# A fused attention and two MLP stages on one core: pooled scores, exponentials, copies, zero products, v pooling and query loads put in another order

## The chip, the core and the metric

The kernel runs on one core of a Trainium2 chip. The metric is the device time of one execution in microseconds, taken as the median of several runs. TensorE is called PE here, its weight loads PEld, VectorE DVE, ScalarE ACT, GpSimd POOL, and SyncE, which issues the loads, SP.

## What is computed

```python
def _attn_ref(q, k, v):            # q, k, v: (2, 8, 576, 64)
    factor = 4; Sd = S // factor   # 144 pooled positions
    q_d, k_d, v_d = (mean over each 4 neighbouring positions of q, k, v)
    out_up = np.repeat(softmax(scale * q_d @ k_d.T) @ v_d, factor, axis=2)
    mask = np.abs(pos[:, None] - pos[None, :]) < factor
    out_local = softmax(where(mask, scale * q @ k.T, -1e9)) @ v
    return out_up + out_local

def reference(...):
    x = attention output as (1152, 512)
    h = x @ w_in                   # 512 -> 2048
    x = (h * clip(h + 3, 0, 6) / 6) @ w_out
    p = domain_probs / domain_probs.sum(-1)
    return sum over 4 experts e of p[:, e] * (relu(x @ w1[e]) @ w2[e])
```

So each head has a local attention (a band of 7 keys) and a pooled one over 144 positions; their sum goes through a gated MLP and then through four dense experts.

## The kernel before, in words

Attention works on 8 units (`Unit`): a unit is one pair of heads of one batch, the two heads on the two halves of the 128 partitions. The loop over `t` (lines 1146 to 1216) is a software pipeline written out by hand: `manual_schedule` keeps the order in which the code issues instructions on every engine, and each engine works its own queue in that order. In turn `t` stand the scores of unit `t`, the turning (transposition by PE) of unit `t-1`, and the products with v of unit `t-2`; the pooling of k and q (`sums`) runs two units ahead.

The steps of a unit, with their lines. `masks` (699): a count of products of zeros (L654, results unused, the count from `IDLE` and `AHEAD_OF`) and the mask as a first product (L703). `scores` (711): 18 windows of 32 queries, 36 matmul instructions (L715). `pooled_scores` (769): L775. `pooled_softmax` (783): DVE takes the maximum (L793, tile mxd) and scales it (L795, nm), ACT does four exponentials with a sum each (L805, eight instructions, tile exd). `less_max` (728): DVE maximum L733 and subtraction L734 (tile ex), ACT exponential L740. `normalise` (742): DVE L745 and L747, POOL multiplies (L749). `pooled_normalise` (814): DVE L816 and L820, POOL multiplies (L821). `turn` (753): PE L759, then ACT copies the result out (L766, L767, tile aT). `pooled_turn` (828): PE L834, ACT copies (L842, tile aTd). `values` (844): 72 matmul instructions (L854). `pooled_values` (863): PE L870, ACT copy pd (L878), DVE sum xf (L884), ACT high part of x (L892); `low` (898): DVE L900. `sums` (661): POOL additions (L510 is the helper's line), for the first units DVE L683.

PSUM: `single()` (163) hands out six banks in turn, so a bank is free again only when what was read from the sixth tile before it has been read; the pooled scores have a double bank of their own (`pair()`). `pool_v(b, idle, cols)` (518) pools half of the columns of v of one batch: `idle` zero products, 36 matmul instructions (L530), two ACT copies (L538). `POOLS` (123) says in which turns; the first half of batch 0 is pooled in turn 1 behind `turn`.

Queries lie in four tiles, and `Q_AT` (48) says which unit uses which; one half of each head's rows must be zero (`clear_q`, 425). Units 0 to 3 get theirs through a loaded slot and two copies (`put_q`, 429; ACT and DVE, lines 421 and 423). Units 4 to 7 are loaded straight into the tile (`load_direct`, 457, four small loads a unit). The loads stand in a list (562 to 586) with the turn from which each may be issued; `load` (196) lets SP wait so that a limited number of bytes is under way. `convert` steps the conversion of the first MLP's weights (227) on ACT and DVE in turns 3 and up. Slots of 8 KB a partition are shared by all of this (`take`, `give`). Two turns after the last unit drain the pipeline (t = 8 and 9), mixed with the first pieces of the MLP (`pieces`, PE lines 410 to 412).

## Time and profile before

| | us |
|---|---|
| median of 3 runs (lowest, highest) | 646.23 (646.16, 647.0) |
| the profiled execution | 647.11 |
| its span in the trace | 645.4 |
| PE busy in the span | 636.8 (99%) |
| DVE busy | 422.4 (65%) |
| ACT busy | 259.5 (40%) |
| POOL busy | 101.2 (16%) |

The attention fills about the first tenth of the span, the two MLPs the rest. In the page's 40 slices PE's busy tenths read 8 in the first, 7 in the last and 9 in all between. The profile's page shows busy shares for the whole span; a share in it is an average over stages with different limits, so what stops the attention has to be read from that stretch alone: from the waits of PE, the order of instructions in time, and the granted clock of PE in each stretch. In the timeline a row gives the start, the time of all instructions merged in the row, engine, line of the code, operation, the tiles written and read, and in brackets the idle time before it with what ended it.

### The profile page before, as it was taken

Reading aid. Unit: us, or ns where it says so; the run is one execution under the profiler, and the core shown is the slowest. Engines: PE = TensorE matmul, PEld = TensorE weight load, DVE = VectorE, ACT = ScalarE, POOL = GpSimd, SP = SyncE. Lnnn points to the kernel's source line nnn. Section 1 sums busy time; section 2 is a strip of 40 time slices with the busy share of each in tenths; the row PEclk is TensorE's granted clock in tenths of the full one; section 3 lists DMA queues with packets and bytes.
Section 4 is the critical chain, followed back from the end, with each engine's and each line's share of the span. In section 5 each row is a group of like instructions: output and inputs, shape, how many; then the busy total and the mean of one; then the engine's idle time right before and its main releaser. Section 6 shows DMA issues by size and latency. Waiting matters only on the chain.

```text
span 645.4 us, 11490 instructions
## 1 busy us (share of the span) xinstructions
PE 636.8 (99%) x4637; PEld 582.6 (90%) x4637; DVE 422.4 (65%) x837; ACT 259.5 (40%) x605; POOL 101.2 (16%) x152
## 2 busy tenths in 40 slices
PE   8999999999999999999999999999999999999997
PEld 4676999999999999998998998998998998988986
DVE  7877899862695238585665665665765755755742
ACT  7767577442564246343223233232341341431310
POOL 5873000000000053201201201201201201201000
PEclk9898999999999999999999999999999999999999
DMA  8876434300420011300110110120210300300012
GB/s 247 207 190 197 133 121 141 131 1 1 171 91 0 1 66 67 131 2 1 66 66 0 67 66 1 66 67 1 72 59 1 113 20 9 123 1 0 2 50 98
DMA packets 24861, 45.86 MB, mean 71 GB/s; under 512 B 11228, under 2 KB 16616, under 8 KB 21352
## 3 DMA queue, kind: packets, MB, share of 16 engines
q1 hardware_dynamic: 24808, 45.13, 21.7%
q8 instruction: 36, 0.59, 0.4%
q14 instruction: 17, 0.14, 0.1%
HBM read 42.76 MB, written 2.36 MB: 70 GB/s over the span
## 4 chain that ended last, share of the span: by engine, by line
PE 93%; DVE 3%; ACT 3%; issue 0%; ACTq 0%; DVEq 0%
PE bank L1051 28%; PE bank L410 10%; PE bank L412 10%; PE bank L411 10%; PE bank L1313 10%; PE bank L1314 10%; PE bank L1312 10%; ACT exd L805 1%; PE pair L854 1%; PE pair L715 1%; PE pair L870 1%; ACT q L421 1%; PE pair L530 1%; DVE mxd L793 1%; PE pair L775 0%; PE pair L654 0%
## 5 line engine op out<-in xcount | busy, mean ns | idle before, releaser
L1051 PEld LDWEIGHTS bank<-xop,slot 128*128 128x128 f32 x1344 | 179.5, 188 | 1.2
L1051 PE MATMUL bank<-xop,slot 128*128 128x288 f32 x1344 | 180.3, 294 | 0.0
L1313 PE MATMUL bank<-slot,h 128*128 128x512 f32 x288 | 112.2, 390 | 0.0
L1312 PE MATMUL bank<-slot,h 128*128 128x512 f32 x288 | 112.1, 389 | 0.0
L1314 PE MATMUL bank<-slot,h 128*128 128x512 f32 x288 | 112.1, 389 | 0.0
L1320 DVE SCALAR_TENSOR_TENSOR slot<-bank,pr,slot 128x512 f32<-128x512 f32 x63 | 47.3, 751 | 80.6 <-PE bank L1314 80.6
L510 POOL TENSOR_TENSOR st<-slot 128x256 f32<-128x256 f32 x16 | 14.0, 872 | 460.8 <-DMA slot<-in_w_dram 231.7
L410 PE MATMUL bank<-x,slot 128*128 128x384 f32 x192 | 64.4, 336 | 0.0
L1314 PEld LDWEIGHTS bank<-slot,h 128*128 128x128 f32 x288 | 54.1, 188 | 11.3
L412 PE MATMUL bank<-x,slot 128*128 128x384 f32 x192 | 64.2, 334 | 0.0
L411 PE MATMUL bank<-x,slot 128*128 128x384 f32 x192 | 64.1, 334 | 0.0
L410 PE MATMUL bank<-h,slot 128*128 128x384 f32 x192 | 64.1, 334 | 0.0
L411 PE MATMUL bank<-h,slot 128*128 128x384 f32 x192 | 64.1, 334 | 0.0
L412 PE MATMUL bank<-h,slot 128*128 128x384 f32 x192 | 64.1, 334 | 0.0
L1312 PEld LDWEIGHTS bank<-slot,h 128*128 128x128 f32 x288 | 54.1, 188 | 10.7
L1313 PEld LDWEIGHTS bank<-slot,h 128*128 128x128 f32 x288 | 54.1, 188 | 10.7
L510 DVE TENSOR_TENSOR u<-bank,u 128x288 f32<-128x288 f32 x96 | 43.6, 454 | 19.7 <-PE bank L1051 19.3
L1080 ACT ACTIVATE h<-c 128x288 fp32r<-128x288 f32 x64 | 27.7, 445 | 71.3 <-DVE c L510 71.3
L340 ACT ACTIVATE slot<-st 128x512 fp32r<-128x512 f32 x32 | 19.2, 626 | 63.2 <-POOL st L334 63.2
L931 ACT ACTIVATE t<-bank,half__190 128x384 f32<-128x384 f32 x48 | 27.7, 582 | 40.3 <-PE bank L412 40.2
L932 DVE SCALAR_TENSOR_TENSOR slot<-t,bank 128x384 f32<-128x384 f32 x48 | 26.3, 552 | 25.1 <-ACT t L931 25.0
L940 DVE TENSOR_TENSOR h<-slot,h 128x384 fp32r<-128x384 f32 x48 | 27.1, 577 | 23.4 <-ACT h L939 23.3
(111 smaller groups left out, 935.3 us busy)
## 6 DMA issues: line engine op xcount, KB each, us to landing
slot<-in_w_dram SPq DMA_DIRECT2D x16, 1024.0 KB, 4.8
slot<-in_w_out_dram SPq DMA_DIRECT2D x8, 1024.0 KB, 4.8
slot<-in_w_in_dram SPq DMA_DIRECT2D x20, 256.0 KB, 4.0
slot<-in_v_dram SPq DMA_DIRECT2D x12, 256.0 KB, 3.8
slot<-in_w_in_dram SPq DMA_DIRECT2D x3, 1024.0 KB, 4.9
slot<-in_kT_dram SPq DMA_DIRECT2D x8, 288.0 KB, 3.3
out_dram<-slot SPq DMA_DIRECT2D x9, 256.0 KB, 2.0
slot<-in_qT_dram SPq DMA_DIRECT2D x4, 288.0 KB, 3.5
```

The lines of the kernel that those rows point to most:

```text
L410: nc.tensor.matmul(ps, wh, xh, start=first, stop=False)
L411: nc.tensor.matmul(ps, wh, xl, start=False, stop=False)
L412: nc.tensor.matmul(ps, wl, xh, start=False, stop=last)
L510: eng.tensor_tensor(out=out, in0=a, in1=b, op=ALU.add)
L931: nc.scalar.activation(out=t, in_=ps, func=AF.Relu, bias=half_, scale=1.0 / (6.0 * UP))
L940: nc.vector.tensor_tensor(out=g[:, 1, :], in0=u, in1=r32(g[:, 0, :]), op=ALU.subtract)
L1051: nc.tensor.matmul(ps, a[:, i, k], b[:, j, k], start=start and k == 0 and n == 0, stop=stop and k == 1 and n == 2, skip_group_check=True,)
L1080: nc.scalar.activation(out=self.h[:, 0, i, j], in_=of, func=AF.Relu)
L1312: nc.tensor.matmul(ps, hh, w[:, 0], start=(f == 0), stop=False)
L1313: nc.tensor.matmul(ps, hh, w[:, 1], start=False, stop=False)
L1314: nc.tensor.matmul(ps, hl, w[:, 0], start=False, stop=(f == NF - 1))
L1320: nc.vector.scalar_tensor_tensor(out=to, in0=ps, scalar=share, in1=to, op0=ALU.mult, op1=ALU.add)
```

## The change

Pooled scores, the maximum of them and the exponentials are split (`pooled_max`, `pooled_exps`). In turns 1 to 7 the pooled scores now stand behind the values of unit `t-2`, the exponentials behind the pooled values, and the high part of x (`high`) behind the exponentials. The pooled normalisation of unit `t-1` moves from the end of its own turn to the following turn, behind `less_max`. `sums` moves to the end of the turn. v's first half is pooled in turn 1 ahead of `turn`, with four zero products in place of two. `AHEAD_OF` gives the mask of turn 2 three zero products, those of turns 4 to 7 one. Units 4 and 5 get their queries through a slot and copies (`pair < 3`), only units 6 and 7 directly, now into tiles 2 and 3; all loads may be issued from the start.

```diff
--- before.py
+++ after.py
@@ -45,7 +45,7 @@
 NWIN = S // QB
 NI = 5
 NA = 2 * NI - 1
-Q_AT = (0, 1, 0, 1, 2, 3, 0, 1)
+Q_AT = (0, 1, 0, 1, 0, 1, 2, 3)
 NP = 3
 W = QB + 2 * (FACTOR - 1)
 WP = 64
@@ -118,11 +118,12 @@
 
 LEFT, RIGHT, BEFORE_H, AFTER = 64, 480, 256, 384
 BEFORE_X = 448
-
-
-POOLS = {4: (0, 1), 6: (1, 0), 7: (1, 1)}
+FIRST_IDLE = 4
+
+
+POOLS = {1: (0, 0), 4: (0, 1), 6: (1, 0), 7: (1, 1)}
 SPARE = {}
-AHEAD_OF = {2: 2, 3: 2, 4: 2, 5: 2, 6: 2, 7: 2, 1: 4}
+AHEAD_OF = {2: 3, 3: 2, 4: 1, 5: 1, 6: 1, 7: 1, 1: 4}
 
 
 JS = 2
@@ -436,7 +437,7 @@
         b, hp = divmod(2 * pair + at, NHP)
         if pair not in k_slots:
             k_slots[pair] = take()
-            if pair < 2:
+            if pair < 3:
                 q_slots[pair] = take()
         k = k_slots[pair][0][:, at * SK : (at + n) * SK].rearrange("p (u s) -> p u s", u=n)
         for edge in (slice(0, FACTOR - 1), slice(SK - FACTOR + 1, SK)):
@@ -468,7 +469,7 @@
 
     def load_qk(pair, at=0, n=2):
         load_k(pair, at, n)
-        if pair < 2:
+        if pair < 3:
             load_q(pair, at, n)
         else:
             load_direct(2 * pair + at)
@@ -574,8 +575,8 @@
         (0, lambda: load_v(0, 0, COLS[1])),
         (0, lambda: load_v(0, 1, COLS[1])),
         (0, lambda: load_v(0, 2, COLS[1])),
-        (3, lambda: load_qk(3, 0, 1)),
-        (4, lambda: load_qk(3, 1, 1)),
+        (0, lambda: load_qk(3, 0, 1)),
+        (0, lambda: load_qk(3, 1, 1)),
         (0, lambda: load_v(1, 0, COLS[0])),
         (0, lambda: load_v(1, 1, COLS[0])),
         (0, lambda: load_v(1, 2, COLS[0])),
@@ -657,6 +658,7 @@
         def __init__(self, u):
             self.u = u
             self.b, self.hp = divmod(u, NHP)
+            self.scale = SCALE / FACTOR**2
 
         def sums(self):
 
@@ -685,7 +687,7 @@
                     two = k2[:, r, : NI - r]
                     add(nc.gpsimd, to, two[:, :, :, 0], two[:, :, :, 1])
             half = k[:, room].rearrange("p (j f) -> p j f", f=2)
-            if pair < 2:
+            if pair < 3:
                 of = q_slots[pair][0][:, o * S : (o + 1) * S].rearrange("p (j f) -> p j f", f=FACTOR)
                 add(nc.gpsimd, half, of[:, :, 0:2], of[:, :, 2:4])
             else:
@@ -722,7 +724,7 @@
 
             if self.u % 2:
                 give(k_slots.pop(self.u // 2))
-                if self.u < NHP:
+                if self.u < 2 * 3:
                     give(q_slots.pop(self.u // 2))
 
         def less_max(self):
@@ -780,9 +782,9 @@
                         stop=True,
                     )
 
-        def pooled_softmax(self):
-
-            scale = SCALE / FACTOR**2
+        def pooled_max(self):
+
+            scale = self.scale
             mx = att.tile([KC, 2, 2], F32, tag="mxd", name="mxd", bufs=2)
             if self.both is None:
                 of = [(mx[:, h], self.sd[h][:KC, : 2 * PK]) for h in range(2)]
@@ -791,7 +793,7 @@
             for to, src in of:
                 src = src.rearrange("p (i w) -> p i w" if src.ndim == 2 else "p h (i w) -> p h i w", w=PK)
                 nc.vector.tensor_reduce(out=to, in_=src, op=ALU.max, axis=AX.X)
-            nm = att.tile([KC, 4], F32, tag="nm", name="nm", bufs=3)
+            self.nm = nm = att.tile([KC, 4], F32, tag="nm", name="nm", bufs=3)
             nc.vector.tensor_scalar(
                 out=nm,
                 in0=mx.rearrange("p h i -> p (h i)"),
@@ -799,6 +801,8 @@
                 scalar2=None,
                 op0=ALU.mult,
             )
+
+        def pooled_exps(self):
             self.exd = att.tile([KC, 4, PK], F32, tag="exd", name="exd", bufs=2)
             self.smd = sm = att.tile([KC, 4], F32, tag="smd", name="smd", bufs=3)
             for n in range(4):
@@ -806,8 +810,8 @@
                     out=self.exd[:, n, :],
                     in_=self.sd[n // 2][:KC, n % 2 * PK : (n % 2 + 1) * PK],
                     func=AF.Exp,
-                    bias=nm[:, n : n + 1],
-                    scale=scale,
+                    bias=self.nm[:, n : n + 1],
+                    scale=self.scale,
                     accum_out=sm[:, n : n + 1],
                 )
 
@@ -889,11 +893,13 @@
                     .to_broadcast([P, n, nj, FACTOR]),
                     op=ALU.add,
                 )
-            nc.scalar.activation(out=hi, in_=self.xf, func=AF.Copy)
             self.hl = hi, lo
             if hp == NHP - 1:
                 for s in v_slots[b].values():
                     give(s)
+
+        def high(self):
+            nc.scalar.activation(out=self.hl[0], in_=self.xf, func=AF.Copy)
 
         def low(self):
             hi, lo = self.hl
@@ -1160,55 +1166,62 @@
                 n.pooled_scores()
                 n.less_max()
                 units[1].sums()
-                n.pooled_softmax()
+                n.pooled_max()
+                n.pooled_exps()
                 n.normalise()
             else:
                 n.masks(AHEAD_OF.get(t, 0))
-                if t == 2:
+                if 1 < t < 2 * 3 - 1:
                     put_q(nc.scalar, t + 1, 0)
                     put_q(nc.vector, t + 1, 1)
-                n.pooled_scores()
                 n.scores()
                 load_next(t + 1)
-                n.pooled_softmax()
-                if t == 1:
-                    units[0].pooled_normalise()
-                    units[2].sums()
                 n.less_max()
+        if 1 <= t <= NU:
+            units[t - 1].pooled_normalise()
+        if t == 1:
+            units[2].sums()
         if 2 < t < NU + 1:
             units[t - 3].low()
         if 0 < t < NU:
             n.normalise()
-            n.pooled_normalise()
         if t == 1:
             put_q(nc.scalar, t + 1, 0)
             put_q(nc.vector, t + 1, 1)
         if t in (1, 2):
-            clear_q(nc.scalar, t + 3, 0)
-            clear_q(nc.vector, t + 3, 1)
-        if 0 < t < NU - 2:
-            units[t + 2].sums()
+            u = 2 * 3 + (1, 2).index(t)
+            clear_q(nc.scalar, u, 0)
+            clear_q(nc.vector, u, 1)
         if t == NU:
             pieces(1)
         if t >= NU:
             units[t - 2].values()
             units[t - 2].pooled_values()
+            units[t - 2].high()
         if t > NU:
             pieces(1)
             units[t - 3].low()
             units[t - 2].low()
         if t in POOLS:
             b, part = POOLS[t]
-            pool_v(b, 0, COLS[part])
+            pool_v(b, FIRST_IDLE if t == 1 else 0, COLS[part])
         if 1 <= t <= NU:
             units[t - 1].turn()
         if 2 <= t < NU:
             units[t - 2].values()
+        if 1 <= t < NU:
+            n.pooled_scores()
+            n.pooled_max()
+        if 2 <= t < NU:
             units[t - 2].pooled_values()
-        if t == 1:
-            pool_v(0, 2, COLS[0])
+        if 1 <= t < NU:
+            n.pooled_exps()
+        if 2 <= t < NU:
+            units[t - 2].high()
         if 1 <= t <= NU:
             units[t - 1].pooled_turn()
+        if 0 < t < NU - 2:
+            units[t + 2].sums()
         convert(3 if t >= NU else {3: 2, 4: 1, 5: 1, 6: 1, 7: 1}.get(t, 0))
         if t in ():
             load_to(loaded[0])
```

## Rows read from the trace of the kernel before

**Rows 1.** Waits of PE, 0 to 72 us: waiter, awaited, total us, times, longest.

```profile
PE pair L654 <- ACT aT L766: 0.6, 2, 0.4
PE pair L854 <- DVE ex L734: 1.1, 1, 1.1
PE pair L715 <- ACT q L421: 0.9, 1, 0.9
PE pair L759 <- POOL ex L749: 0.5, 1, 0.5
```

**Rows 2.** Timeline of PE in turn 5: start, us, engine, line, operation.

```profile
38.02 0.60 PE L654 MATMUL pair<-zeros 128*128 128x512 bf16 x2
38.46 0.31 PE L703 MATMUL pair<-mask,identb 128*128 128x342 bf16 x1
38.70 0.71 PE L775 MATMUL pair<-slot 64*72 64x144 f32 x8
39.34 1.25 PE L715 MATMUL pair<-slot,q 128*64 128x38 f32 x36
40.52 0.76 PE L759 MATMUL pair<-ident,ex 128*128 128x128 f32 x5
41.21 1.35 PE L854 MATMUL pair<-aT,slot 38*64 38x32 f32 x72
42.50 0.86 PE L870 MATMUL pair<-aTd,slot 80*64 80x144 f32 x8
43.29 0.70 PE L834 MATMUL pair<-ident,exd 72*80 72x72 f32 x8
43.97 0.59 PE L654 MATMUL pair<-zeros 128*128 128x512 bf16 x2
```

**Rows 3.** Timeline of PE in turns 1 and 4.

```profile
8.55 1.04 PE L654 MATMUL pair<-zeros 128*128 128x512 bf16 x4
...
13.49 1.93 PE L530 MATMUL pair<-slot,fours 38*32 38x256 f32 x36
...
28.83 0.91 PE L654 MATMUL pair<-zeros 128*128 128x512 bf16 x2 [0.38 <-ACT aT L766]
...
32.86 1.93 PE L530 MATMUL pair<-slot,fours 38*32 38x256 f32 x36
```

**Rows 4.** Stretches: length, busy PE, PEld, DVE, ACT, POOL; PE clock; DMA share; GB/s.

```profile
28.80:31.00 2.20, 2.17 (x11) 1.04 (x10) 1.99 (x7) 1.10 (x4) 1.68 (x2) 0.54 0.73 194
38.00:44.00 6.00, 6.00 (x144) 4.54 (x143) 5.47 (x10) 3.76 (x15) 3.56 (x6) 1.00 0.71 201
52.50:55.50 3.00, 3.00 (x21) 1.71 (x19) 2.45 (x5) 2.00 (x6) 1.74 (x2) 0.56 0.81 262
```

**Rows 5.** Chain that ended last, in turn 5: start, us, what.

```profile
40.11 0.68 DVE mxd L793
...
41.51 1.55 ACT exd L805 x8
43.06 0.39 ACT ex L740
```

**Rows 6.** Timeline of POOL, DVE and ACT, turns 2 to 5.

```profile
16.96 0.98 POOL L749 TENSOR_TENSOR ex<-ex,rec 128x342 f32<-128x342 f32 x1
19.01 2.56 POOL L510 TENSOR_TENSOR slot<-slot 128x288 f32<-128x288 f32 x5
22.22 0.99 DVE L423 CAST q<-zeros 64x576 f32<-64x576 bf16 x1
24.00 0.48 DVE L492 MEMSET slot<- 3x512 f32 x1
45.35 0.68 ACT L892 ACTIVATE x<-xf 128x576 fp32r<-128x576 f32 x1 [1.10 <-DVE xf L884]
45.94 0.68 ACT L842 ACTIVATE aTd<-pair 80x288 f32<-80x288 f32 x2
```

**Rows 7.** Timeline of SP's queue: the first loads of v.

```profile
2.70 5.10 SPq L198 DMA_DIRECT2D slot<-in_v_dram  x9
```

**Rows 8.** The page's DMA issues: count, size, median us from issue to landing.

```profile
slot<-in_v_dram SPq DMA_DIRECT2D x12, 256.0 KB, 3.8
```

## The prediction, made before the changed kernel ran

> **What bounds the kernel now.** I read the page first: TensorE (PE) is busy almost through the whole span and the chain of work that ended last runs on it. Behind the attention the two MLPs keep PE at nine tenths or more of every slice but the last, so only the first slices, the eight turns of attention, are open. There I read three views. The waits of PE up to 72 us [rows 1] name what stopped it: 1.1 us once in the middle of the value products (L854) for DVE's subtraction L734, 0.6 us in two pieces at a turn's first zero product (L654) for the copy L766, 0.5 us at L759 and 0.9 us at the very start (L715). The timeline of turn 5 [rows 2] shows a turn that nothing stopped: two zero products 0.44 us, mask 0.24, scores 1.18 (L715), turn 0.69 (L759), values 1.29 (L854), pooled values 0.79 (L870), pooled turn 0.68 (L834), and pooled scores 0.64 (L775): 5.95 us from 38.02 to 43.97. So a turn is bound by PE's own work, and what can be won is only what lies above these 5.95 us. The third view, the stretches with their granted clock [rows 4], shows the rest: twice the clock is near half of full (0.54 at 28.8 us, 0.56 at 52.5 us), so the lower of the two levels, 1.2 instead of 2.4 GHz. Each time PE had just stood still: 0.38 us ahead of the 28.83 us product [rows 3], and the 1.1 us of [rows 1] shortly before 52.5 us. What one fall costs is read from turn 4: from its first zero product to the end of its scores it takes 32.86 - 28.83 = 4.03 us [rows 3], in turn 5 the same work takes 40.52 - 38.02 = 2.50 us [rows 2]: 1.5 us a fall, 3.0 us for two.
>
> **The change part by part.**
>
> *Pooled scores behind the values.* The turn's first bank is freed by the copies L766, and in the kernel before these stand in ACT's queue behind eight exponential steps that need the pooled scores of the same turn. In the new order ACT's local exponential and L766 come first. PE does as much as before. The two waits for L766 (0.6) go, since those copies now need nothing later than the scores. The 1.1 us wait for L734 goes: in the kernel before DVE had the pooled maximum and its scaling (together 41.51 - 40.11 = 1.40 us to the first exponential, [rows 5]) ahead of the maximum and subtraction of the scores; both now stand behind the subtraction. The 0.5 us at L759 goes because v is now pooled ahead of the first turn: that work, 1.93 us long [rows 3], fills the time in which the normalised exponentials come. Removed: 0.6 + 1.1 + 0.5 = 2.2 us. The 0.9 us at the start stay.
>
> What comes in their place has three parts.
>
> (a) *The pooled normalisation L821 and its reader are now in one turn.* POOL is in order: L749(1), then the sums of unit 3, then L821 of unit 1. L749 begins at 16.96 and takes 0.98, the five sums take 2.56, and L821 some 1.07 (it is what lies between the end of L749 at 17.94 and the sums at 19.01) [rows 6]: 16.96 + 0.98 + 2.56 + 1.07 = 21.57. PE: from 8.55 [rows 3] four zeros 0.88, mask 0.24, scores 1.18, four zeros 0.88, pooling 1.9, turn 0.69, pooled scores 0.64, pooled turn 0.68: 15.6; then three zeros 0.66, mask 0.24, scores 1.18, turn 0.69, values 1.29, pooled scores 0.64, pooled values 0.79: 21.1 is where the pooled turn of unit 1 wants L821. So a wait of 0.5, less whatever PE is late by. Bounds 0 (PE late by as much) to 1.0 (POOL late by as much again); I take 0.3, since (c) makes PE some 0.2 late. In later turns L821 waits for DVE's denominators, which stand behind the subtraction: with 1.40 for the maximum and what follows it (an estimate, by the pooled maximum of [rows 5]) and 1.07 it is done 2.5 us after the scores, PE asks for it 0.69 + 1.29 + 0.64 + 0.79 = 3.4 us after them: no wait, 0.9 us to spare.
>
> (b) *The second bank of the values is freed by the first copy L842 of the pooled turn one turn earlier*, which now stands last on ACT. From the pooled scores' end: maximum to last exponential 43.06 - 40.11 = 2.95 us [rows 5], the copy to x (L892, behind it now) some 0.6, half of the two copies L842 0.34 [rows 6]: 3.9. PE from the same point: pooled values 0.79, pooled turn 0.68, one or two zeros 0.22 or 0.44, mask 0.24, scores 1.18, turn 0.69: 3.8 or 4.0. So nothing to spare, in the turns without pooling of v, 3 and 5 (in 4, 6 and 7 the pooling gives 1.9 us more). In turn 3 the clearing of a query tile (0.99, [rows 6]) stands ahead of that maximum on DVE. Bounds 0 to 1.0 together (below nothing can't be: it is a wait); I take 0.4, nearest to the half of the clearing.
>
> (c) *v pooled ahead of the first turn.* PE asks for v at 8.55 + 0.88 + 0.24 + 1.18 + 0.88 = 11.7. The nine loads are issued by 7.8 and such a load lands 3.8 after its issue [rows 7, 8]: 11.6. The wait is 0 at least and 13.49 - 11.7 = 1.8 at most, since at 13.49 the kernel before did this work without a wait [rows 3]. I take 0.2.
>
> *Fewer zeros.* Counted from the tables: before 11 + 4 + 6 x 2 + 2 = 29 zero products, after 11 + 4 + 4 + 3 + 2 + 4 x 1 = 28. One at 0.22 us [rows 2]: 0.2 us less. The last four turns have one each and no more; what that does to the clock is weighed below.
>
> *Direct loads for the last queries alone, all loads issued at the start.* Units 4 and 5 get their queries through a slot and two copies each (ACT and DVE, in turns 3 and 4), in place of eight small direct loads. PE has no wait for a load in [rows 1], so earlier loads win nothing there; and the copies stand at a turn's head, ahead of a subtraction that is waiting for scores, where both engines are idle: nothing on PE. Without that cover each would delay L766 by some 0.7 us, as long as the copy L892 of the same size [rows 6], and in these turns there is more than that to spare. On POOL the sums of units 4 and 5 become whole-width ones: no longer than those of unit 3. The slots' edges of the last pair are filled at the start on POOL, ahead of the constants, and two fills of v's slots (0.48 each, [rows 6]) on DVE ahead of the mask: that part of PE's start has the 0.9 us wait for the queries behind it, so 0 to 0.1; I take 0. On SP no issue waits for scores any more.
>
> **The sum** against the profiled execution, 647.11 us with a span of 645.40: removed 2.2 of waits, 0.2 of zeros, 3.0 of low clock if it never falls; added 0.3 + 0.4 + 0.2 = 0.9. That is -4.5. The waits that stay are of the length of the 0.38 us pause ahead of the fall at 28.8 us, and the one in turn 3 stands among the value products, as the 1.1 us pause did. So I keep one fall, +1.5: **-3.0 us**, 644.1 for such a profiled execution. The median of the runs is 646.23, 0.9 below the profiled one; taken off there as well: **643.2**. What is won before 62 us reaches the end if the weights' conversion keeps up: it hangs on PE's last turns and moves along with them.
>
> **The clock, and what the Trainium skill says of it.** The row that speaks for less cover: from 38.0 to 44.0 PE ran without a pause, from 39.3 on without a zero product [rows 2], and the clock stayed at 1.00 [rows 4]. The Trainium skill, "TensorE: Matmul & The Clock Gate", Part 1, "What's actually happening", says that the low clock is the default and that activity releases it; that speaks against taking zero products out. In the same page "A second HAM failure mode: psum-queue depth-cycling" says that short idles between groups of matmuls, as PSUM banks are cycled, make the clock swing; by that the falls go with the waits. By the first alone the sum would end at rival 2, by the second at rival 1.
>
> **The rivals.** (1) *No fall at all*: the three remaining waits are too short. -4.5: 641.7. For: of the two pauses at L654, 0.6 us together, the shorter brought no fall [rows 1]. Against: the longer, 0.38, did [rows 3]. (2) *The clock falls oftener (slower).* With one zero product in each of the last four turns, a short wait anywhere in a turn brings the clock down, as the 0.38 us did. Each fall costs 1.5, so three eat the 4.5 and it decides from the fourth: 646.23 - 4.5 + 6.0 = 647.7; five give 649.2. For: both falls began in a turn's stretch from the values to the next zero products. Against: the stretch from 38 to 44 us [rows 2, 4]. (3) *A new wait in each turn takes the place of the old ones*: L821 or L842 is late by 0.5 in six turns, and both falls stay: 2.2 + 0.2 go, 3.0 come, 646.8. For: (b) has nothing to spare. Against: PE's being late gives time to the others, so that such a wait doesn't add up. (4) *Two falls as before*, -1.5: 644.7. That the loads' part does nothing is in the sum already.
>
> **How the numbers follow.** One fall left, 643.2: 0.34. None, 641.7: 0.28. Two, 644.7: 0.15. Three falls or new waits, about 646.2 to 646.8: 0.11. Slower by the clock, 647.7 and up: 0.12. A measurement of this kernel can tell 0.2% (1.3 us) from no change: faster is the first three less a little, 0.75; same 0.13; slower 0.12. The range: downwards all that is removed and none of the added waits, 646.23 - 5.4 = 640.8; upwards to 646.0, which takes in two falls with the upper bounds of (a) and (b), and leaves out the last two cases.
>
> **What would show it.** Right: in the waits of PE L654 for L766 and L854 for L734 are gone; PE's first MLP product comes some 3 us earlier; at most one stretch of half clock before it; short waits at L834 for L821 and at L854 for L842. Wrong: a longer wait for v at L530; three or more stretches of half clock; a wait of 0.5 us for L842 or L821 in each turn; a wait of PE behind 72 us for a converted weight.

## The result, and the profile after

The changed kernel takes 642.87 us (median of 20 executions, 641.96 to 670.23); the kernel before, run beside it, 652.35 (20 executions, 644.57 to 657.12). The ratio is 0.9887, with a 95% interval from 0.9849 to 0.9924. It is a ratio of means, and like the ratios further down it leaves out each execution that is more than 1.5% above the fastest of its kernel: here all 8 of the changed kernel above 650 us (655.83 to 670.23), but only 2 of the 11 of the kernel before. Over all 20 executions each, the means are 652.1 and 650.5. So the usual execution became faster, the mean of all did not.

Both medians hide a spread that the three runs ahead of the prediction (646.16 to 647.0) did not show: single executions of either kernel differ by how long the granted clock of PE stays at its lower level (at a mean clock of 1.00 the kernel before takes 644.60 to 644.75, at 0.995 646.9 to 647.5, at 0.984 653.6 to 654.0), so each comparison below says which clock it is at. At 1.00 the changed kernel takes 641.94 to 642.54 in most executions: 644.60 - 641.94 = 2.7 us less from lowest to lowest.

The profile that came with the result is of an execution of 670.23 us, with a long stretch of low clock. The same kernel profiled once more took 641.94 us, with a span of 640.2 and PE busy for 632.5 of it; that one stands against the profiled execution of before (647.11, span 645.4). From turn 1's first zero product to the first MLP product it takes 56.89 - 8.79 = 48.10 us; in the kernel before it was 62.18 - 8.55 = 53.63 (8.55 in [rows 3]; 62.18 is the start of its first product at L410). So 5.5 us are won there, 0.24 are lost ahead of it, and the span is 5.2 shorter. The profiled execution of before has its two falls of the clock in that stretch [rows 4], this one has none.

The waits of PE up to 110 us in the profile of 641.94 us (waiter, awaited, total, times, longest), for [rows 1]:

```profile
PE pair L655 <- DVE zeros L558: 1.3, 1, 1.3
PE pair L705 <- DVE mask L627: 0.8, 1, 0.8
PE pair L838 <- POOL exd L825: 0.7, 1, 0.7
PE pair L838 <- DVE nm L797: 0.4, 1, 0.4
PE pair L761 <- POOL ex L751: 0.3, 1, 0.3
PE pair L655 <- issue: 0.2, 1, 0.2
```

The first row, at the start, is in the view of before too (L654 for L557, 1.3), though [rows 1] leaves it out. Lines have moved by one to four: zeros are L655, mask L705, scores L717, turn L761, pooled scores L777, pooled turn L838, values L858, pooled values L874; on POOL, L751 and L825 are the two normalisations. The waits for the copy behind L654, for the subtraction in the middle of the values, and half a microsecond for the first L749 are gone. New are two at the pooled turn, 0.4 in turn 2 and 0.7 in turn 5, and 0.3 at L761 in turn 2. The timeline of the same execution, turn 5 and the two ends of the count above, for [rows 2, 3]:

```profile
8.79 0.81 PE L655 MATMUL pair<-zeros 128*128 128x512 bf16 x3 [0.16 <-issue]
...
35.63 0.38 PE L655 MATMUL pair<-zeros 128*128 128x512 bf16 x1
...
36.09 1.25 PE L717 MATMUL pair<-slot,q 128*64 128x38 f32 x36
36.34 2.12 DVE L284 SCALAR_TENSOR_TENSOR slot<-slot 128x512 f32<-128x512 uint32 x2
37.27 0.77 PE L761 MATMUL pair<-ident,ex 128*128 128x128 f32 x5
37.96 1.35 PE L858 MATMUL pair<-aT,slot 38*64 38x32 f32 x72
38.38 0.50 DVE L735 TENSOR_REDUCE mx<-pair 128x9 f32<-128x342 f32 x1
39.25 0.71 PE L777 MATMUL pair<-slot 64*72 64x144 f32 x8
39.89 0.86 PE L874 MATMUL pair<-aTd,slot 80*64 80x144 f32 x8
39.96 1.48 POOL L825 TENSOR_TENSOR exd<-exd,recd 72x576 f32<-72x576 f32 x1 [1.22 <-ACT ex L742]
41.49 0.70 PE L838 MATMUL pair<-ident,exd 72*80 72x72 f32 x8 [0.74 <-POOL exd L825]
42.03 0.38 PE L655 MATMUL pair<-zeros 128*128 128x512 bf16 x1
...
56.89 0.42 PE L411 MATMUL bank<-x,slot 128*128 128x384 f32 x1
```

The turn takes 42.03 - 35.63 = 6.40 us, of which 0.74 are the new wait: 5.66 of work, against 5.95 with one zero product (0.22) more before. The granted clock is 1.00 in every stretch of this execution. In the one of 670.23 us it is not. Its stretches (length, busy PE, PEld, DVE, ACT, POOL; clock; DMA share; GB/s), for [rows 4]:

```profile
24.00:26.00 2.00, 1.18 (x9) 0.64 (x9) 1.94 (x5) 1.57 (x9) 0.74 (x2) 1.00 0.79 244
26.00:28.00 2.00, 1.10 (x42) 1.10 (x44) 1.50 (x5) 2.00 (x6) 0.84 (x1) 0.62 0.86 266
28.00:80.00 52.00, 52.00 (x704) 35.81 (x702) 23.22 (x55) 22.88 (x76) 18.38 (x27) 0.50 0.52 148
84.00:86.00 2.00, 2.00 (x8) 2.00 (x8) 1.05 (x3) 1.08 (x3) 1.43 (x1) 0.50 0.00 0
88.00:90.00 2.00, 2.00 (x61) 1.56 (x54) 0.34 (x1) 0.29 (x1) 0.00 (x0) 1.00 0.00 0
```

In a pause that ends at 26.90 us the clock falls (the 0.62 of 26:28 puts it at about 26.5), and PE works at 0.50, the lower of its two levels (1.2 GHz), until 87.5 us: all the rest of the attention, and 4.6 us on from the first MLP product at 82.94. PE is busy without a gap there, 52.00 of 52.00 us. In [rows 4] a fall lasted some 3 us. The pause, in the timeline of the same execution:

```profile
20.33 1.15 POOL L825 TENSOR_TENSOR exd<-exd,recd 72x576 f32<-72x576 f32 x1
20.41 2.73 DVE L424 CAST q<-zeros 64x576 f32<-64x576 bf16 x1
...
23.06 0.74 DVE L795 TENSOR_REDUCE mxd<-pair 72x4 f32<-72x576 f32 x1
...
26.90 2.15 PE L858 MATMUL pair<-aT,slot 38*64 38x32 f32 x68 [1.48 <-ACT aTd L846]
```

DVE's clearing of a query tile in turn 2 (L424) took 2.73 us, the pooled maximum came 2.3 us later than in the other execution (20.72 there), with it the pooled exponentials and the copy L846, and the values (L858) stood for 1.48 us. In the execution of 641.94 us there is no wait at L858, and the same instruction reads:

```profile
20.40 1.40 POOL L825 TENSOR_TENSOR exd<-exd,recd 72x576 f32<-72x576 f32 x1
20.40 0.39 DVE L424 CAST q<-zeros 64x576 f32<-64x576 bf16 x1
20.72 0.75 DVE L795 TENSOR_REDUCE mxd<-pair 72x4 f32<-72x576 f32 x1
```

0.39 against 2.73 us for one instruction. Where POOL's product starts 0.08 us ahead, DVE waits out that product and POOL's next one (L751, up to 22.20); where both start together, DVE goes through and POOL is the longer one (1.40 against 1.15). The Trainium skill, "SBUF — State Buffer", section "Who interferes with whom", has a rule that says this: casts and copies of DVE in their faster mode and GpSimd shut each other out of a shared port pair for a whole instruction, and the order of issue decides who waits. The two traces agree.

### The profile page after: what moved, and what is told of

Read it like the earlier page. It is cut to its first block, busy times and chain, and to the rows that moved or that the text cites. A ratio compares the mean times of both kernels' runs of the same rounds, so it can differ in the third digit from the quotient of the medians.

```text
span 668.5 us, 11463 instructions
## 1 busy us (share of the span) xinstructions
PE 660.7 (99%) x4633; PEld 598.6 (90%) x4636; DVE 421.8 (63%) x839; ACT 260.5 (39%) x607; POOL 99.2 (15%) x150
## 4 chain that ended last, share of the span: by engine, by line
PE 96%; ACT 2%; DVE 2%; issue 0%; ACTq 0%; DVEq 0%
PE bank L1057 27%; PE bank L411 10%; PE bank L412 10%; PE bank L413 10%; PE bank L1326 10%; PE bank L1325 10%; PE bank L1327 10%; PE pair L858 2%; PE pair L531 2%; PE pair L717 1%; PE pair L874 1%; PE pair L838 1%; PE pair L777 1%; PE pair L761 1%; ACT exd L809 1%; DVE q L424 1%
## 5 line engine op out<-in xcount | busy, mean ns | idle before, releaser
L411 PE MATMUL bank<-x,slot 128*128 128x384 f32 x192 | 65.2, 340 | 0.0
L412 PE MATMUL bank<-x,slot 128*128 128x384 f32 x192 | 64.9, 338 | 0.0
L413 PE MATMUL bank<-x,slot 128*128 128x384 f32 x192 | 64.9, 338 | 0.0
```

What stands on the lines that cost most here:

```text
L411: nc.tensor.matmul(ps, wh, xh, start=first, stop=False)
L412: nc.tensor.matmul(ps, wh, xl, start=False, stop=False)
L413: nc.tensor.matmul(ps, wl, xh, start=False, stop=last)
```

## Experiments

**The changed kernel once more**, unedited, for a profile beside that of the result.

> The changed kernel itself once more, to see an execution whose clock does not stay low. In the profile at hand PE waits 1.48 us in the value products of turn 3 (L858) for the copy L846, and the clock falls right there and stays at the lower level up to 87 us. If that wait belongs to the kernel, it is in this profile too, 1.3 to 1.6 us long, with the clock at 1.00 behind it, and the span is near 640.3. If it belongs to that execution, the wait is under 0.5 us, as the prediction had it (0.4).

Measured: 641.94, 642.01, 642.29 and 655.79 us; the profile shown above. The wait of 1.48 us is not in every execution: at 641.94 us there is none at L858. Together with the result's 20 executions, 9 of 24 are above 650 us and the other 15 between 641.94 and 644.51. Those 9 have a mean clock of 0.95 to 0.976, 14 of the 15 one of 0.999 or 1.00. So there are two questions: what the change is worth with the clock up, and how often the clock stays down.

**The clearing of the last query tiles one turn earlier** (turns 0 and 1 in place of 1 and 2).

```diff
-        if t in (1, 2):
-            u = 2 * 3 + (1, 2).index(t)
+        if t in (0, 1):
+            u = 2 * 3 + t
```

> The clearing of the query tiles of units 6 and 7 one turn earlier (turns 0 and 1 in place of 1 and 2), nothing else. Theory A: the wait of 1.48 us in turn 3 comes from DVE's clearing in turn 2, which lasts 2.73 us beside POOL's products (0.99 in the kernel before) and holds up the pooled maximum; then the wait falls to 0.3 us or less, the undisturbed time to about 640.5, and no execution falls to the lower clock for long. Theory B: ACT's row of exponentials, high part and copies is itself too long by that much (term b of the prediction, with nothing to spare); then a wait of 0.5 us or more stays in turn 3 and the time moves by under 0.8 us.

Measured: 642.49 to 643.04 us in five executions (clock 0.998 to 1.00), 644.59 to 645.65 in four (0.996 or 0.997), 666.26 in one (0.958); ratio 0.991 (0.9863 to 0.9957). The timeline in turn 2, of an execution of 643.04 us:

```profile
20.59 1.14 POOL L825 TENSOR_TENSOR exd<-exd,recd 72x576 f32<-72x576 f32 x1
21.69 0.76 POOL L751 TENSOR_TENSOR ex<-ex,rec 128x342 f32<-128x342 f32 x1
21.70 1.40 DVE L797 TENSOR_SCALAR nm<-mxd 72x4 f32<-72x4 f32 x1
21.79 0.70 PE L838 MATMUL pair<-ident,exd 72*80 72x72 f32 x8
25.66 1.25 PE L858 MATMUL pair<-aT,slot 38*64 38x32 f32 x68 [0.49 <-ACT aTd L846]
```

The long clearing is gone, but a multiplication of four numbers a partition (L797, 0.17 us where POOL is idle, as at 10.57 us in the trace of before) now takes 1.40 us beside POOL's products, and L858 still waits 0.49. So it is not the size of DVE's operation, and not that one clearing: the cast and the scaling both paid POOL's length. Not every form did: the maximum L795 took 0.75 within POOL's 1.40 in the rows above. Neither theory came out as put. 0.49 of the wait is left where A allowed 0.3, and no execution came near A's 640.5: the lowest is 0.5 above that of the changed kernel.

**Two zero products in each turn** (the table of before, four ahead of turn 1 alone), to see whether they keep the clock.

```diff
-FIRST_IDLE = 4
+FIRST_IDLE = 2
-AHEAD_OF = {2: 3, 3: 2, 4: 1, 5: 1, 6: 1, 7: 1, 1: 4}
+AHEAD_OF = {2: 2, 3: 2, 4: 2, 5: 2, 6: 2, 7: 2, 1: 4}
```

> The changed kernel with the counts of zero products of the kernel before (two in each of turns 2 to 7, two ahead of the first pooling of v): 29 in place of 28. If the zero products only cost their own time, the undisturbed time is 642.2, within 0.3 of the changed kernel, and executions whose clock falls still lose 14 to 28 us. If one a turn is too little to bring the clock back once it fell, as rival 2 fears, the long stays at the lower level are gone: no execution above 650.

Measured: five executions from 642.44 to 642.81 us, one of 656.33, four from 671.08 to 675.68. The clock in the profiled one, of 675.68 us:

```profile
23.00:68.00 45.00, 44.12 (x606) 31.41 (x610) 20.16 (x48) 19.58 (x65) 18.84 (x30) 0.50 0.69 194
```

With two in each turn the clock stays down about as often as with one, 5 of 10 against 9 of 24: two do not hold it.

**All but the order**: the kernel before with the loads, the counts of zero products and the place of v's pooling of the change.

```diff
-Q_AT = (0, 1, 0, 1, 2, 3, 0, 1)
+Q_AT = (0, 1, 0, 1, 0, 1, 2, 3)
...
-AHEAD_OF = {2: 2, 3: 2, 4: 2, 5: 2, 6: 2, 7: 2, 1: 4}
+AHEAD_OF = {2: 3, 3: 2, 4: 1, 5: 1, 6: 1, 7: 1, 1: 4}
...
-            pool_v(b, 0, COLS[part])
+            pool_v(b, FIRST_IDLE if t == 1 else 0, COLS[part])
...
```

> The kernel before with all of the change but the order of the pooled steps: loads and query tiles, zero counts and v pooled ahead of the first turn. By the prediction's sum the order takes out 0.6 + 1.1 us of waits and v's place 0.5; so this one keeps waits of L654 for L766 and of L854 for L734, 1.2 to 1.7 us in all, loses the 0.5 at L759, and gains 0 to 1 us on the kernel before. If the order brought nothing, it is as fast as the changed kernel, 4 us ahead of the one before. With one zero product a turn its clock may fall oftener than before: then it is slower by 1.5 us for each further fall.

Measured: 646.32, 660.81, 660.85 and 662.19 us, none at full clock (646.32 has 0.995), so there is no ratio. In the profile (660.81 us) the wait in the middle of the values is still there:

```profile
PE pair L855 <- DVE ex L735: 0.9, 1, 0.9
```

at 34.40 us (50.42 in the trace of before), and the clock is at 0.50 from 36 to 76 us, so later waits can't be compared. With the new order only one profile has a like wait, that with a conversion step moved (below). So the removal of this wait belongs to the order, as the prediction had it, and the long stays do not: they come with the old order too.

**The scaling nm on ACT**, with the earlier clearing, so that neither of DVE's two operations meets POOL there.

```diff
-            nc.vector.tensor_scalar(
-                out=nm,
-                in0=mx.rearrange("p h i -> p (h i)"),
-                scalar1=-scale,
...
+            nc.scalar.activation(
+                out=nm, in_=mx.rearrange("p h i -> p (h i)"), func=AF.Copy, scale=-scale
+            )
```

> The changed kernel with the clearings one turn earlier (as in the run before) and the scaling nm of the pooled maximum on ACT in place of DVE. In the run with the earlier clearing alone, DVE's nm, a product over 72 x 4 values, lasted 1.40 us in turn 2 beside POOL's L825 and L751, and PE still waited 0.5 us at L858. Theory A, DVE's clearing and scaling are held up by POOL's products: with neither of them left in that place the wait of L858 for the copy L846 is gone (0.1 us or less), and the lowest time is near that of the changed kernel (641.9) or up to 0.5 below. Theory B, ACT's row itself is too long: ACT has one more instruction of some 0.2 us in that row now, so the wait at L858 is 0.5 to 0.8. Under both PE still waits 0.4 to 0.7 for POOL's L825 at L838 in turn 2.

Measured: 641.37, 641.47, 641.86, 642.05, 642.24 and three of 655.1 to 655.3 us; ratio 0.9903 (0.9849 to 0.9957). The wait at the values is gone from the trace, and the lowest time is 0.6 under that of the changed kernel. The 0.4 to 0.7 us that were expected to stay in turn 2 are not in the view of waits either: POOL's product takes 1.14 there, with neither of DVE's two operations beside it, instead of 1.40. One pause is left, in turn 5, and as it ends the clock falls. Its timeline, of an execution of 655.13 us (the pooled turn is L834 here):

```profile
40.87 1.18 PE L834 MATMUL pair<-ident,exd 72*80 72x72 f32 x8 [0.59 <-POOL exd L821]
```

and its stretches:

```profile
42.00:68.00 26.00, 26.00 (x344) 16.83 (x342) 11.27 (x25) 11.47 (x37) 7.75 (x10) 0.50 0.65 206
72.00:73.00 1.00, 1.00 (x47) 0.75 (x49) 0.00 (x0) 0.55 (x1) 0.17 (x1) 1.00 0.00 0
```

Again PE is busy without a gap at the lower level, from 41 to 71.5 us, and again it comes back some us behind the first MLP product, which starts at 68.83 us here. That costs 655.1 - 641.9 = 13 us.

**The sums a turn later**, on top of the last run, to take both pauses away: `sums` of each unit from unit 3 on stands one turn later, off POOL's queue ahead of the pooled normalisation.

```diff
-        if 0 < t < NU - 2:
-            units[t + 2].sums()
+        if 1 < t < NU - 1:
+            units[t + 1].sums()
```

> As the last one, and the sums of a unit one turn later (unit t+1 at the end of turn t), so that in turn 1 POOL has one unit's sums ahead of the pooled normalisation in place of two. The prediction's term a (0.3, bounds 0 to 1.0) is the wait of L838 for L825 that the two units' sums make. If that is its cause, the wait in turn 2 is gone and the lowest time falls by 0.3 to 0.7 us to 641.2 to 641.6; the waits of PE between 10 and 57 us are then under 0.5 us in all. If pauses bring the clock down, hardly an execution loses more than 2 us; if it is the sequence of PE's work without a pause, the executions above 650 stay as frequent as with the changed kernel (8 of 21).

Measured: 641.42 to 643.89 in nine executions, 663.47 in one; ratio 0.9936 (0.9903 to 0.9969). The wait of turn 5 is 0.34 us instead of 0.59, and PE stands 1.2 us at another place for nothing that the profile shows. The lowest time is that of the run before it, whose view had no wait in turn 2 any more that could have been won. Whether pauses start the stays is left open: 1 of 10 against 3 of 8 is no difference in so few.

**The order alone**: the new order, with the loads, the counts of zero products and v's place of the kernel before.

```diff
-                n.pooled_scores()
                 n.scores()
...
+            n.pooled_scores()
+            n.pooled_max()
...
+            n.pooled_exps()
```

> The new order of the pooled steps alone, in the kernel before: loads, query tiles, zero counts and the place of v's first pooling are those of the kernel before. The prediction puts 1.7 us of removed waits on the order (L654 for L766, L854 for L734) and up to 0.7 of new ones: an execution at full clock should be at 643 to 644.2, against 644.6 for the kernel before and 641.9 for the changed one. If the order carries all of the gain it is at 642.

Measured: 668.71, 672.84 and 678.59 us; ratio 1.0414 (1.0322 to 1.0506), slower than before. The stretches of the profiled execution (672.84 us):

```profile
16.00:20.00 4.00, 3.76 (x83) 2.94 (x84) 3.68 (x7) 2.39 (x12) 3.69 (x8) 1.00 0.84 162
20.00:24.00 4.00, 4.00 (x84) 2.82 (x76) 3.00 (x7) 3.18 (x10) 3.42 (x9) 0.80 0.94 263
24.00:88.00 64.00, 64.00 (x814) 44.70 (x813) 29.47 (x69) 27.63 (x96) 22.28 (x34) 0.50 0.46 124
```

The clock falls at about 22.4 us (0.80 in 20:24), in a stretch in which PE was busy all the time; the last pauses ahead of it are 0.24 us at 19.63 and 1.45 at 12.37. It stays down to about 90 us; the other two executions have mean clocks of 0.956 and 0.938, so long stays as well. So no long pause right ahead is needed for a fall, and what the order alone is worth at full clock was not seen.

**The loads' part undone** in the changed kernel: tiles, loads and copies of the queries as before.

```diff
-Q_AT = (0, 1, 0, 1, 0, 1, 2, 3)
+Q_AT = (0, 1, 0, 1, 2, 3, 0, 1)
...
-            if pair < 3:
+            if pair < 2:
...
-        (0, lambda: load_qk(3, 0, 1)),
-        (0, lambda: load_qk(3, 1, 1)),
+        (3, lambda: load_qk(3, 0, 1)),
+        (4, lambda: load_qk(3, 1, 1)),
...
```

> The changed kernel with the query tiles and loads of the kernel before (units 4 to 7 loaded directly, the last pair's loads held to turns 2 and 3). The prediction puts nothing on this part: an execution at full clock within 0.5 us of the changed kernel's 641.9. Rival: the whole-width sums of units 4 and 5 give POOL time, and without them L825 comes late in turns 3 and 4; then PE waits 0.3 us or more at L838 in those turns and the time is 0.5 to 1.5 us longer.

Measured: six executions from 643.19 to 644.16 us, three above 655; ratio 0.9921 (0.9873 to 0.997). The lowest is 1.2 us above that of the changed kernel. The waits of PE, of an execution of 644.14 us:

```profile
PE pair L531 <- DMA slot<-in_v_dram: 1.4, 3, 0.6
PE pair L838 <- POOL exd L825: 0.4, 1, 0.4
```

and the second and the last of the three waits for v in its timeline:

```profile
31.43 1.51 PE L531 MATMUL pair<-slot,fours 38*16 38x256 f32 x28 [0.65 <-DMA slot<-in_v_dram]
...
46.40 1.51 PE L531 MATMUL pair<-slot,fours 38*16 38x256 f32 x28 [0.58 <-DMA slot<-in_v_dram]
```

1.4 us of waits for loads of v that neither the kernel before nor the changed one has: a PE that comes earlier meets the old loads before they have landed. The rival, POOL's L825 late in turns 3 and 4, is out: its only wait, 0.4, is in turn 2.

**One conversion step less in turn 4, one more in turn 6**, on the run with nm on ACT, so that no step stands ahead of the maximum in turn 5.

```diff
-        convert(3 if t >= NU else {3: 2, 4: 1, 5: 1, 6: 1, 7: 1}.get(t, 0))
+        convert(3 if t >= NU else {3: 2, 5: 1, 6: 2, 7: 1}.get(t, 0))
```

> The kernel with the earlier clearing and the scaling on ACT, and the weight conversion's steps shifted: none in turn 4, one in turn 5, two in turn 6 (before: one in each). In the profiles of the changed kernel and its two variants PE still waits 0.3 to 0.7 us at the pooled turn of turn 5 for POOL's L821/L825; there DVE is at the conversion (L284, 2.12 us beside POOL, 1.3 alone) when the scores are ready, so the maximum starts 0.7 us late. Theory A, the conversion step in turn 4 makes that wait: it is under 0.2 us now, and the lowest time 0.3 to 0.6 us below 641.4. Theory B, POOL's own queue makes it: it stays. If a pause of PE is what starts a fall of the clock, executions above 650 get rarer than 3 of 8.

Measured: 642.0 and 643.09 us at a clock of 1.00, 644.95 to 647.31 in eight executions at 0.992 to 0.994, 653.12 and 654.47 in two at 0.981 and 0.978; median 646.04, ratio 0.9945 (0.99 to 0.9989). The wait of turn 5 is gone, as the theory that blamed the step has it. The waits of PE, of an execution of 646.89 us, show others in turn 7:

```profile
PE pair L834 <- issue: 1.5, 1, 1.5
PE pair L854 <- DVE den L816: 1.1, 1, 1.1
```

For the second, the timeline has another conversion step on DVE (L263, 1.29 us from 52.20 on) ahead of the maximum and the subtraction of the scores. The work is only moved to a turn that has as little room for it, and short falls came in eight of twelve executions. At full clock the lowest time, 642.0, is no better than without the move (641.37).

**Four zero products in each turn.**

```diff
-AHEAD_OF = {2: 3, 3: 2, 4: 1, 5: 1, 6: 1, 7: 1, 1: 4}
+AHEAD_OF = {2: 4, 3: 4, 4: 4, 5: 4, 6: 4, 7: 4, 1: 4}
```

> The changed kernel with four zero products ahead of the mask in each of turns 2 to 7: 15 more than its own count, 3.3 us of PE's time at 0.22. At full clock that makes 645.2. With two a turn executions at 656 to 676 stayed as frequent as with one, so zero products as such did not bring the clock back. If a longer dense stretch at the head of a turn does, no execution is above 650 and all lie within 2 us of 645.2. If what keeps the clock low is the order of the products behind the mask, executions above 655 stay.

Measured: 644.16 to 644.3 us in eleven executions, 645.8 in one; ratio 0.994 (0.9905 to 0.9975). No long stay in twelve, and the profile has 1.00 in each stretch. The price: 15 products more for 644.18 - 641.96 = 2.2 us, 0.15 each. That is net: one takes 0.22 [rows 2], and some of them fill waits (the 0.7 of turn 5 is gone from the view).

**v pooled behind the turn again**, with its four zero products.

```diff
-POOLS = {1: (0, 0), 4: (0, 1), 6: (1, 0), 7: (1, 1)}
+POOLS = {4: (0, 1), 6: (1, 0), 7: (1, 1)}
...
+        if t == 1:
+            pool_v(0, FIRST_IDLE, COLS[0])
```

> The changed kernel with the first pooling of v back behind the turning of unit 0, its four zero products with it. The prediction puts 0.5 us on this part (the wait at L759/L761 in turn 1 for POOL's L749/L751) less 0.2: an execution at full clock at 642.2 to 642.5, against 641.95. In the run with the new order alone PE waited 1.5 us at L761 in turn 2 and then stayed at the lower clock in each of its executions; if v's place is what guards against that, the wait is there again and most executions are above 655. If it is not, the waits are 0.5 in turn 1 and under 0.5 in turn 2, with long stays no more frequent than in 9 of 25.

Measured: six executions from 642.56 to 643.32 us, one of 647.36, five above 656; ratio 0.9911 (0.9859 to 0.9962). Lowest against lowest, the place of v is worth 0.6 us. In the timeline of an execution of 642.59 us:

```profile
12.39 0.77 PE L761 MATMUL pair<-ident,ex 128*128 128x128 f32 x5 [1.45 <-POOL ex L751]
```

The wait is in turn 1, as in the run with the order alone (12.37 there), but the clock is 1.00 in every stretch of this execution, and 5 of 12 is hardly more frequent than 9 of 24. So nothing shows that v's place guards the clock, and a pause of 1.45 us need not bring it down.

**Three zero products in each turn, nm on ACT, the clearing earlier**: the cheapest count that might hold the clock, on the quickest order.

```diff
-AHEAD_OF = {2: 3, 3: 2, 4: 1, 5: 1, 6: 1, 7: 1, 1: 4}
+AHEAD_OF = {2: 3, 3: 3, 4: 3, 5: 3, 6: 3, 7: 3, 1: 4}
```

> The kernel with the earlier clearing and the scaling on ACT, with three zero products ahead of the mask in each of turns 2 to 7 (9 more than the changed kernel). With four of them the changed kernel was at 644.2 in nearly every execution and never above 646; with two, half of its executions were above 655. The lowest time here: 641.4 for this kernel plus 9 x 0.15 to 9 x 0.22, less what waits they fill: 642.0 to 643.4. If three a turn suffice, no execution is above 650 and the middle one is at 642.5 to 643.5, so ahead of both kernels over all executions. If four are needed, some are at 655 or above, as with the same kernel at one a turn (3 of 8).

Measured: twelve executions, 642.64 to 643.28 us, median 642.79; the kernel before beside it 648.28 (17 executions), ratio 0.991 (0.9872 to 0.9948). The waits of PE up to 80 us, and two of the stretches:

```profile
PE pair L655 <- DVE zeros L558: 1.3, 1, 1.3
PE pair L705 <- DVE mask L627: 0.5, 1, 0.5
PE pair L531 <- DMA slot<-in_v_dram: 0.4, 1, 0.4
```

```profile
28.00:42.00 14.00, 14.00 (x321) 10.04 (x319) 10.89 (x24) 10.45 (x38) 10.88 (x16) 1.00 0.67 152
42.00:57.00 15.00, 14.62 (x341) 10.00 (x340) 10.93 (x25) 11.40 (x39) 8.25 (x10) 1.00 0.80 240
```

No new wait at L834 or L854 is left. It is not the lowest time (642.64 against 641.37 with one product a turn), but it has no long stay: its mean is 642.88, that of the kernel before beside it 648.99, that of the changed kernel's 24 executions 651.0.

## Why the prediction was right, and where its steps were not

It said 643.2 us, between 640.8 and 646.0; the median is 642.87. The sign and the main mechanism held: the waits that the order was to take out are gone. That the number is so near is in part luck. The prediction took 3.0 us off 646.23 and kept one short fall of the clock. Measured side by side the medians differ by 9.5 us and at full clock the lowest times by 2.7, and an execution of the changed kernel has, in place of one short fall, mostly next to none or a long stay.

- **Removed waits, 2.2 us: right in kind, too small.** All three are gone. That the subtraction's goes with the order is shown by the run of all but the order, which keeps 0.9 us of it; that the turn's goes with v's place, by v pooled behind the turn, where 1.45 us come back (more than the 0.5 of [rows 1], since the pooled scores no longer stand ahead of it) and the time rises by 0.6. The wait for the copy L766 was read too small, 0.6 instead of 1.4 us; how is shown behind this list.
- **(a) L825 and its reader in one turn: right in turn 2, wrong in turn 5.** Turn 2 has 0.4 us where 0.3 was taken. The row names DVE's nm, but L838 starts at 21.85, just behind L825 (20.40 and 1.40 long); with the earlier clearing it starts at 21.79, behind L825 and long before nm has ended. The step that failed is "In later turns ... no wait, 0.9 us to spare": it had DVE take up the maximum when the scores are there. In turn 5 a conversion step on DVE (L284, 2.12 us) ran from 36.34 on, the maximum began at 38.38, 2.3 us after the scores began, and L825 took 1.48 instead of 1.07: 0.74 us of wait. Moving the step away took this wait away. The 0.3 us at L761 in turn 2, for POOL's L751, had no term.
- **(b) the values' second bank: right in mechanism, too small in its bound.** 0 in the execution of 641.94 us, 1.48 in that of 670.23; the bound was 1.0. The clearing was priced at 0.99 from [rows 6]; it is 0.39 or 2.73, by who starts first. That it was this wait's cause is shown by moving it and nm off DVE's path: the wait goes.
- **(c) v's landing: 0**, inside its bounds; 0.2 was taken.
- **Start: right in what it named.** The wait of 0.9 us for the queries has become one of 0.8 for the mask, which the two fills on DVE stand ahead of; the scores of unit 0 begin at 6.75 us instead of 6.73. The first zero product of turn 1 still comes 0.24 later (8.79 instead of 8.55), behind a pause of 0.16 at issue, which no step had.
- **Loads: predicted 0, measured 1.2 us.** The step was "PE has no wait for a load in [rows 1], so earlier loads win nothing there". It read the waits of a slower PE; with the other parts in, the old loads cost 1.4 us in three waits.
- **The clock: "I keep one fall, +1.5" failed.** In 14 of 24 executions there is next to none (mean clock 0.999 or more), and the time is rival 1's, which put it at 641.7; 13 of them lie between 641.94 and 642.57. In one there are short falls, and in 9 a stay that costs 14 to 28 us. The price was read from falls that ended after some 3 us [rows 3, 4]; the trace of before gave no reason why they end, and none was asked for. As the price of a short fall it was near: the kernel before takes 647.11 with its two falls and 644.60 without, 1.3 each instead of 1.5. The kernel before has stays as well, but shorter ones, and takes no more than 657.17: of 88 executions whose clock is known 41 are above 650 us, all at 0.976 to 0.987, most at 0.984, which is some 2 x 0.016 x 645 = 21 us at 0.50 (an estimate from the mean). The longer stays eat the gain: the mean of all 24 executions of the changed kernel is 651.0, of 108 of the kernel before 650.0. So the ratio of 0.9887 is neither the gain at full clock (2.7 us, 0.4%) nor that over all executions (none); it depends on how often, and for how long, each kernel's executions fell into a stay.
- **The size at full clock: too small by 1.2 us.** The sum without its clock terms is -1.5; measured at 1.00 it is -2.7. With the loads' part undone the lowest time is 643.19, so the rest is worth 1.4, near the predicted 1.5; but two errors meet there, the wait for L766 (0.8 too small) and the 1.4 us of waits for v that stand in that run and not in the sum. In the two traces compared above no wait for a load stands on either side; there the wait for L766 is the term mis-sized most, and the new waits go the other way, 1.4 us instead of 0.9. A trace of the kernel before at full clock was not kept, and that the parts add up was not shown, since the order alone never ran at full clock.
- **The tail: right.** 5.5 us won up to the first MLP product less 0.24 lost at the start are 5.3; the span is 5.2 shorter.

**The wait for L766, from start to start.** The view of waits counts idle time only from the modelled end of L834 (0.70 us long in its row), and of the four waits that follow here it lists two. Where nothing holds it, PE starts the next zero product 0.53 or 0.54 us after it started L834: so at the end of each turn in the new trace (41.49 to 42.03 above). In the trace of before it is 0.95, 0.85, 1.08 and 0.68 at the ends of turns 1, 2, 3 and 5, and each time L766 ended 0.04 to 0.05 us ahead of the zero product. Less 0.53 each, that is 1.4 us of waiting. Rows of two of these ends, from the trace of before (43.29 and 43.97 stand in [rows 2]):

```profile
21.65 0.70 PE L834 MATMUL pair<-ident,exd 72*80 72x72 f32 x8
21.85 0.60 ACT L766 ACTIVATE aT<-pair 128x512 f32<-128x512 f32 x1
22.50 0.59 PE L654 MATMUL pair<-zeros 128*128 128x512 bf16 x2
...
43.33 0.59 ACT L766 ACTIVATE aT<-pair 128x512 f32<-128x512 f32 x1
```

So even the turn that the prediction takes as one "that nothing stopped" waited 0.15 us for L766, which it counts into the 0.68 of the pooled turn. With the order alone the end of turn 1 takes 0.54 in place of 0.95: this wait goes with the order.

**What holds the clock.** Executions above 650 us, by zero products in a turn. One, in turns 4 to 7: 9 of 24 (changed kernel), 3 of 8 (nm on ACT), 1 of 10 each (clearing earlier; sums later), 5 of 12 (v behind the turn), 3 of 9 (old loads), 2 of 12 (conversion moved), 3 of 4 (all but the order). Two: 5 of 10, 3 of 3 (order alone) and 52 of 108 (all executions of before). Three: 0 of 12. Four: 0 of 12. Three or four kept it up here, two did not. Three were tried on one variant alone, and what they do was not told apart: they are work without a pause, and they also give the helpers time, so that the pause of turn 5 is gone with them.

What starts a fall stays open. In three profiles it came within, or 0.4 us behind, a pause of 1.48, 0.59 or 0.40 us, in two others 1.5 to 2.7 us behind one of 0.94 or 0.24, in that of before 0.2 and 2.4 us behind 0.38 and 1.11; but profiles with a pause of 1.45 (v behind the turn), 1.17 (sums later) or 0.74 (turn 5 above) kept 1.00. The Trainium skill, "TensorE: Matmul & The Clock Gate", Part 1, "What's actually happening", says that the low clock is the default and activity releases it. For that, the zero products count; against it taken plainly, PE without a gap for 52 us at 0.50 in the result's profile.

## What to carry to other kernels

When an order is changed so that the bounding engine comes earlier, ask anew of every load and every helper engine whether it still comes in time: "no wait in the trace" holds only for the old pace. Keep casts and scalings on DVE away from POOL's products where either is on the path; on ACT the scaling cost its own length (0.21 us). Where an engine's clock can fall, look at many executions before pricing a fall, and weigh the cheap work that holds it (here 0.15 us a product) against the mean of the times, not against the best: by the mean the changed kernel wins nothing as it stands, with three products in a turn and the two operations off DVE's path 6 us. And read a wait also from start to start: a view that counts from a modelled end can hide part of it.

## What was not expected of the hardware

One DVE cast of 64x576 took 0.39 or 2.73 us, as POOL's product started at the same time or 0.08 us earlier; a scaling of 72x4 took 0.17 or 1.40. A fall of PE's clock from 2.4 to 1.2 GHz lasted some 3 us in the profile of before, 7 in another and 30 to 75 in five more, with PE busy almost throughout (52.00 of 52.00 us, 44.12 of 45.00); those five ended 1 to 12 us behind the first MLP product. The times of one unchanged kernel on one core went by this from 644.44 to 657.17 us in 108 executions, those of the changed one from 641.94 to 670.23 in 24.
